# A second order of steps for a gated linear attention followed by a rational feed-forward layer

## The chip, the cores and the metric

One core of one Trainium2 chip. The metric is the device time of one execution in microseconds, lower is better. The profile is of one execution; the other runs are timed without it.

## The reference

The kernel computes an attention with a decaying state, and a two-layer feed-forward network on its output with a rational activation between the layers. Cut to what matters:

```python
# 4 batches x 8 heads, 768 positions, head size 48
f = 1.0 / (1.0 + np.exp(-f_logit))
for t in range(S):
    state = f[:, :, t, :, None] * state + np.einsum('bhd,bhe->bhde', k[:, :, t], v[:, :, t])
    y[:, :, t] = np.einsum('bhd,bhde->bhe', q[:, :, t], state)
x = y.transpose(0, 2, 1, 3).reshape(3072, 384)
h = x @ w_in                                   # 384 -> 2048
P = a[0] + a[1] * h + a[2] * h**2 + a[3] * h**3
Q = 1.0 + np.abs(b[0]) * np.abs(h) + np.abs(b[1]) * h**2
out = (P / (Q + 1e-06)) @ w_out                # 2048 -> 384
```

Inputs and output are float32 in HBM.

## The kernel before

**Units.** The work is cut into 12 units of 256 positions of one batch: unit n is batch n mod 4 and third n div 4 of the sequence. A state is carried from the unit of a batch to its next one, four units on. A step is one piece of work of a unit on one engine. Its name stands first, then the unit, then which part: heads by groups of two, or columns of the 2048 by blocks of 128. A last `@i` is the PSUM slot that a step's output takes; there are four slots of two banks each.

**Steps of the attention half.** `ld n f|k|q|v` loads an input of a unit: f, k and q from the queue of SP as float32 (L200, 384 KB each), v from the queue of POOL, cast to bf16. `ef` and `ls` (ACT, L308 and L313) make the exponential and the logarithm of the gate, `cs` (PE, L323) its sum over positions, `A n 1` and `A n 0` (ACT, L332) the exponentials of that sum, `xa n 1` and `xa n 0` (DVE, L337) multiply k and q by them. `T` (PE, L348) transposes both, `Te` (DVE, L356) reads that out of PSUM, `sc` (PE, L369) makes the scores, `mk` (DVE, L377) masks them, `vm` (POOL, L388; for unit 0 ACT) copies a part of v, `sv` and `id` (PE, L413 to L428) make the new state, `ae` (ACT, L461) and `st` (DVE, L465) finish it, `yb` (PE, L394) makes the output of the attention, and `ye` (ACT, L456) reads it out as the input of the second half.

**Steps of the feed-forward half.** `h` (PE, L474) is the first matmul, in four blocks of 512 columns, each in one PSUM slot. `hy` (ACT, L488) reads it out, `sq` (DVE, L492) or `sa` (ACT, L496) squares it, `ab` (DVE, L500) takes the absolute value. The two terms of Q are added either on PE, `u` (L508) with the logarithm `ln` (ACT, L516) behind it, or by an accumulating transfer from POOL's queue, `zd` (L525) with the logarithm `lz` (ACT, L532). `ex` (ACT, L540) makes 1/Q. `p1`, `p2` and `pm` (DVE, L545, L550, L555) make the pieces of P, which are added by an accumulating transfer from POOL's queue, `ta` (L559), or on DVE, `tv` (L563). `gm` (DVE, L568) multiplies by 1/Q. `o` (PE, L581) is the second matmul, `oe` or, for the last unit, `oc` (L596, L604) reads it out, and `so`, `s0`, `s1` (L590) store it. `wi` and `wo` (POOL's queue, L216, L220) load the weights, cast to bf16; `hv` (DVE, L210) is a small write that `wi` has to wait for. `cz`, `cc`, `ca`, `cb`, `fa`, `fb` make constants.

**What sets the order.** One text, ORDER (from L19), lists all 829 steps, and a loop at the end of the kernel issues them in that order. No scheduler moves them: each engine, and each queue of transfers, runs its own steps in the order in which they stand in the text, and a step waits until its inputs are written and its buffer is free. A step that waits holds up all behind it on its engine or queue. Buffers: three of each of f, k, q and v, two or three of the large arrays of the second half, one of most of the attention's arrays.

Of the kernel before, what the change touches and what calls it, by code (L numbers as in the profile page):

```python
# [19 lines left out]
b1_; cz 0; cb; ca; ld 0 f 2 4; ld 0 f 0 2; ld 0 q 2 4; cc; ld 0 k 2 4; cz 1; ld 0 k 0 2; fa 0  # L20
ef 0 2 4; ld 0 q 0 2; ls 0 2 4; ef 0 0 2; cs 0 2 4 @0; ld 0 v; cz 3; ls 0 0 2; A 0 1 2 4; ld 1 f
cs 0 0 2 @1; cz 2; A 0 0 2 4; A 0 1 0 2; xa 0 1 2 4; A 0 0 0 2; ld 1 k; xa 0 0 2 4; rg; hv 0
xa 0 1 0 2; T 0 2 4 @1; wi 0 4; ld 1 q; xa 0 0 0 2; id 0 0 @0; Te 0 2 4; T 0 0 2 @2; vc 0; ab_
wi 4 8; vm 0 0 s; Te 0 0 2; ae 0; sc 0 0 @2; sc 0 1 @1; sv 0; ef 1; ld 2 f; ld 1 v; ls 1; st 0 0
wi 8 16; mk 0 1; id 0 1; vm 0 1 s; cs 1 @3; mk 0 0; A 1 1; yb 0 0 4 @2; A 1 0; xa 1 1; st 0 1
id 1 0 @3; ye 0; fa 1; ld 2 q; h 0 0 4 @2; ld 2 k; xa 1 0; fb; T 1 @0; hy 0 0 4; h 0 4 8 @1; ae 1
Te 1; sc 1 0 @0; hy 0 4 8; sc 1 1 @2; mk 1 0; ld 3 f; ef 2; sv 1; vm 1 0; sq 0 0 8; ls 2; ld 2 v
cs 2 @0; ab 0 0 8; ld 3 v; mk 1 1; u 0 0 4 @1; A 2 1; vm 1 1; A 2 0; st 1 0; u 0 4 8 @2; p1 0 0 8
ln 0 0 4; id 1 1; h 0 8 12 @0; p2 0 0 8; ld 3 q; ln 0 4 8; pm 0 0 8; yb 1 0 4 @2; ex 0 0 8; xa 2 0
h 0 12 16 @1; st 1 1; ld 3 k; ye 1; tv 0 0 8; hy 0 8 12; h 1 4 8 @2; xa 2 1; hy 0 12 16; vm 2 0  # L30
id 2 0 @0; gm 0 0 8; wo 8 12; hy 1 4 8; sv 2; ld 4 f; vm 2 1; h 1 0 4 @1; sq 0 8 16; ae 2; sa 1 4 8
wo 0 4; wo 4 8; ef 3; p1 0 8 16; h 1 12 16 @2; wo 12 16; hy 1 0 4; st 2 0; ab 0 8 16; vm 3 1; id 2 1
ld 4 q; sa 1 0 4; T 2 @3; ab 1 0 8; vm 3 0; ld 4 v; st 2 1; ls 3; u 1 0 4 @1; Te 2; hy 1 12 16
cs 3 @0; pm 0 8 16; ln 1 0 4; u 0 12 16 @3; A 3 1; sc 2 0 @2; p2 0 8 16; h 1 8 12 @1; A 3 0; mk 2 0
ln 0 12 16; sc 2 1 @0; xa 3 1; u 0 8 12 @2; ld 5 f; hy 1 8 12; ld 4 k; mk 2 1; u 1 4 8 @3; ef 4
id 3 0 @1; ln 0 8 12; ab 1 8 16; yb 2 0 4 @0; xa 3 0; ls 4; sv 3; ld 5 v; p1 1 0 16; ye 2; T 3 @2
ln 1 4 8; o 0 0 0 4 @0; Te 3; ex 0 8 16; cs 4 @3; o 0 1 0 4; tv 0 8 16; h 2 0 4 @2; A 4 0; sq 1 8 16
A 4 1; o 0 1 4 8; sa 2 0 4; gm 0 8 16; h 2 4 8 @3; ld 6 f; ae 3; ld 5 q; hy 2 0 4; pm 1 8 16
o 0 1 8 12; hy 2 4 8; h 2 12 16 @2; pm 1 0 8; ex 1 0 8; st 3 0; o 0 0 4 8; p2 1 0 16; id 3 1
o 0 1 12 16; hy 2 12 16; o 0 0 8 12; st 3 1; ta 1 0 8; sa 2 4 8; xa 4 1; sc 3 0 @1; sc 3 1 @2  # L40
vm 4 1; o 0 0 12 16; ef 5; ld 7 f; mk 3 0; ld 5 k; h 2 8 12 @3; ef 6; mk 3 1; ld 6 q; oe 0 0 2 s
u 1 8 12 @1; hy 2 8 12; ab 2 0 8; yb 3 0 4 @2; xa 4 0; ls 5; u 1 12 16 @3; vm 5 1; ab 2 8 16
ln 1 8 12; vm 4 0; sq 2 8 16; T 4 @0; zd 2 0 8; ln 1 12 16; so 0 0 2; cs 5 @1; ta 1 8 16; ye 3; Te 4
u 2 12 16 @3; A 5 0; p1 2 0 16; sv 4 @0; A 5 1; sc 4 1 @2; ex 1 8 16; h 3 0 4 @1; mk 4 1; ld 6 k
p2 2 0 16; h 3 4 8 @2; hy 3 0 4; gm 1 0 8; ln 2 12 16; id 4 0; u 2 8 12 @1; ae 4; hy 3 4 8; xa 5 0
h 3 12 16 @3; ls 6; st 4 0; xa 5 1; ef 7; id 4 1; ld 8 f; h 3 8 12 @2; st 4 1; hy 3 12 16; pm 2 0 8
sv 5 @0; ln 2 8 12; sc 4 0 @3; id 5 0; ta 2 0 8; hy 3 8 12; mk 4 0; o 1 0 0 4 @1; ae 5; o 1 0 4 8
lz 2 0 8; st 5 0; cs 6 @3; ab 3 0 8; pm 2 8 16; o 1 1 0 4; A 6 0; yb 4 0 4 @2; gm 1 8 16; ta 2 8 16
A 6 1; id 5 1; o 1 1 4 8; ex 2 0 8; sq 3 0 8; o 1 0 8 12; o 1 1 8 12; p1 3 0 16; zd 3 0 8; ye 4
T 5 @3; ld 6 v; ex 2 8 16; st 5 1; h 4 0 4 @2; Te 5; ld 7 v; ld 9 f; ld 7 k; o 1 0 12 16; vm 5 0  # L50
pm 3 0 8; ld 7 q; hy 4 0 4; h 4 4 8 @3; sa 4 0 4; xa 6 0; o 1 1 12 16; ab 3 8 16; sa 4 4 8
h 4 8 12 @2; gm 2 0 8; hy 4 4 8; sq 3 8 16; h 4 12 16 @0; oe 1 0 2 s; hy 4 8 12; gm 2 8 16
o 2 0 0 4 @1; hy 4 12 16; sc 5 0 @2; xa 6 1; sc 5 1 @3; o 2 0 4 8; ls 7; mk 5 0; o 2 1 0 4; lz 3 0 8
cs 7 @0; ab 4 0 8; ld 10 f; u 3 8 12 @2; so 1 0 2; mk 5 1; A 7 1; o 2 1 4 8; ln 3 8 12; p2 3 0 16
yb 5 0 4 @3; A 7 0; sv 6 @2; ab 4 8 16; ld 8 k; ta 3 0 8; ye 5; o 2 0 8 12; pm 3 8 16; ex 3 0 8
# [12 lines left out]
sc 7 0 @2; hy 6 0 4; o 4 0 0 4 @1; mk 7 0; sa 6 0 4; o 4 1 0 4; o 4 0 4 8; mk 7 1; ex 5 8 16; T 8 @3
sq 6 8 16; yb 7 0 4 @0; ls 9; p1 6 0 16; u 6 12 16 @2; ld 10 v; ye 7; lz 5 0 8; o 4 1 4 8; ab 6 0 8
Te 8; o 4 1 8 12; h 7 4 8 @0; ln 6 12 16; pm 6 8 16; ex 5 0 8; h 7 0 4 @3; gm 5 8 16; vm 9 0  # L70
ld 10 q; zd 6 0 8; ld 10 k; o 4 0 8 12; p2 6 0 16; so 3 0 2; hy 7 4 8; o 4 0 12 16; vm 9 1; cs 9 @2
hy 7 0 4; gm 5 0 8; ta 6 8 16; sc 8 1 @0; A 9 0; o 4 1 12 16; sq 7 0 8; A 9 1; h 7 12 16 @3; mk 8 1
oe 4 0 2 s; ef 10; sc 8 0 @2; ld 11 q; sv 8 @1; pm 6 0 8; id 8 0; hy 7 12 16; u 6 8 12 @0; mk 8 0
ls 10; ta 6 0 8; h 7 8 12 @3; ae 8; ln 6 8 12; xa 9 1; cs 10 @2; hy 7 8 12; st 8 0; o 5 0 0 4 @0
ab 7 0 8; ex 6 8 16; yb 8 0 4 @3; xa 9 0; zd 7 0 8; sv 9 @1; sq 7 8 16; id 9 0; ye 8; o 5 1 0 4
p1 7 0 16; ae 9; A 10 0; o 5 1 4 8; ef 11; T 9 @3; st 9 0; ld 11 k; ab 7 8 16; A 10 1; h 8 12 16 @1
Te 9; zd 7 8 16; lz 6 0 8; h 8 8 12 @2; pm 7 8 16; hy 8 12 16; xa 10 1; o 5 0 4 8; hy 8 8 12
sc 9 1 @3; p2 7 0 16; sc 9 0 @1; o 5 1 8 12; so 4 0 2; ls 11; h 8 4 8 @2; mk 9 0; ex 6 0 8
ta 7 8 16; ld 11 v; mk 9 1; o 5 0 8 12; o 5 1 12 16; hy 8 4 8; ab 8 8 16; o 5 0 12 16; sa 8 4 8
# [565 lines left out]
```

## Time and profile before

| what | value |
|---|---|
| median of 3 runs (lowest, highest) | 220.58 us (219.79, 221.02) |
| the profiled execution, its own time | 221.11 us |
| its span in the profile | 219.4 us |
| busy: PE, DVE, ACT, POOL | 201.3, 203.7, 200.7, 76.3 us |
| weight loads of PE | 142.9 us |
| moved by DMA | 42.86 MB, 195 GB/s on average |
| HBM read, written | 25.17 MB, 4.72 MB |

Three engines are busy for 91 to 93% of the span, so a share over the whole span tells little: what matters is where the rest lies, and which wait stands on the way of which engine. The granted TensorE clock is full nearly throughout. Busy PE time counts each matmul from its issue to the end of its pipeline, and is not the same as a full PE. An engine "waits" in this profile when it is idle before an instruction; the name behind the arrow is what ended the wait.

### The profile page before, as it was taken

The page shows a single profiled execution, that of the slowest core. Times are in us where ns is not written, and L with a number is a line of the kernel's source. Part 1 is how long each engine was busy: PE and PEld are TensorE (multiplying, and loading weights), DVE is VectorE, ACT ScalarE, POOL GpSimd, SP SyncE. Part 2 cuts the span into 40 slices and gives each one's busy share as a digit, 9 for nine tenths or more (in the row PEclk, how much of TensorE's full clock was granted, in tenths as well). Part 3 has the DMA queues.
Part 4 walks back from the last instruction along what each step waited for, and adds up shares of the span by engine and source line. Part 5 has one row for each costly group of instructions (what it writes and reads, how often), then busy time and mean ns, then how long its engine had stood idle before and what let it go on. Part 6 is the DMA issues. An engine that isn't in the chain of part 4 may idle for free.

```text
span 219.4 us, 7100 instructions
## 1 busy us (share of the span) xinstructions
PE 201.3 (92%) x3106; PEld 142.9 (65%) x3120; DVE 203.7 (93%) x249; ACT 200.7 (91%) x215; POOL 76.3 (35%) x95
## 2 busy tenths in 40 slices
PE   1569599999999999999999999999999999999991
PEld 1447377567757778577668676786867776865450
DVE  4768999999999999999999999999999999999951
ACT  5554799999999999999999999999999999999980
POOL 4472419020261149362906533123423303231000
PEclk9999999999999999999999999999999999999999
DMA  5999999999999899699999999976978998999515
GB/s 141 266 200 214 225 224 189 207 198 244 268 218 239 226 207 155 129 264 191 214 246 253 215 269 200 214 135 127 193 150 157 193 203 160 187 200 188 112 45 143
DMA packets 62128, 42.86 MB, mean 195 GB/s; under 512 B 51474, under 2 KB 57362, under 8 KB 62098
## 3 DMA queue, kind: packets, MB, share of 16 engines
q0 software_dynamic: 19792, 23.14, 64.3%
q1 hardware_dynamic: 42144, 19.08, 34.8%
q8 instruction: 24, 0.39, 0.7%
q10 hardware_dynamic: 162, 0.20, 0.3%
q14 instruction: 6, 0.05, 0.1%
HBM read 25.17 MB, written 4.72 MB: 136 GB/s over the span
## 4 chain that ended last, share of the span: by engine, by line
PE 40%; ACT 28%; DVE 18%; issue 6%; DMA 2%; SPq 2%; ACTq 0%; DVEq 0%
PE hp L474 15%; PE op L581 13%; ACT hy L488 6%; ACT qi L540 6%; PE y L394 3%; DVE h L492 3%; ACT A L332 3%; ACT h L496 3%; ACT lq L516 3%; DVE gall L568 3%; DVE z L500 2%; PE u L508 2%; DMA fn<-in_f_logit_dram 2%; SPq L200 2%; PE tp L348 2%
## 5 line engine op out<-in xcount | busy, mean ns | idle before, releaser
L581 PE MATMUL op<-w_out_sb,gall 128*128 128x384 bf16 x384 | 69.8, 326 | 0.1
L474 PE MATMUL hp<-xT,w_in_sb 128*128 128x256 bf16 x576 | 68.8, 273 | 0.8 <-ACT xT L456 0.4
L474 PEld LDWEIGHTS <-w_in_sb 128*128 128x128 bf16 x576 | 55.6, 98 | 11.1 <-issue 1.7
L488 ACT CAST hy<-hp 128x1024 bf16<-128x1024 f32 x48 | 49.2, 1063 | 3.3 <-PE hp L474 3.2
L581 PEld LDWEIGHTS <-gall 128*128 128x128 bf16 x384 | 36.2, 98 | 23.4 <-DVE gall L568 1.1
L540 ACT ACTIVATE qi<-lq 128x2048 bf16<-128x2048 f32 (+1 forms) x25 | 46.6, 1888 | 0.1
L559 POOL DMA_DIRECT2D gall<-hy x21 | 20.1, 959 | 66.7 <-DVE gall L555 18.7
L388 POOL COPY vmp<-vn 128x128 bf16<-128x128 bf16 x22 | 26.1, 1198 | 14.3 <-DMA vn<-in_v_dram 10.9
L568 DVE TENSOR_TENSOR gall<-gall,qi 128x2048 bf16<-128x2048 bf16 (+1 forms) x25 | 29.6, 1184 | 1.5 <-ACT qi L540 1.3
L377 DVE TENSOR_TENSOR scm<-sc,mask 128x1024 bf16<-128x1024 f32 x24 | 28.8, 1216 | 0.7 <-PE sc L369 0.5
L555 DVE TENSOR_TENSOR gall<-gall,h 128x2048 bf16<-128x2048 bf16 (+1 forms) x25 | 29.2, 1172 | 0.0
L532 ACT ACTIVATE lq<-z 128x2048 f32<-128x2048 bf16 x13 | 25.5, 1974 | 0.0
L516 ACT ACTIVATE lq<-u 128x1024 f32<-128x1024 f32 x22 | 23.3, 1067 | 0.2 <-PE u L508 0.2
L332 ACT ACTIVATE A<-cs 128x768 f32<-128x768 f32 (+1 forms) x26 | 19.2, 791 | 3.4 <-PE cs L323 3.3
L492 DVE TENSOR_TENSOR h<-hy 128x2048 bf16<-128x2048 bf16 (+1 forms) x18 | 20.9, 1158 | 0.0
L525 POOL DMA_DIRECT2D z<-h x13 | 13.1, 1014 | 21.1 <-ACT osb L596 4.7
L500 DVE TENSOR_SCALAR z<-hy 128x2048 uint16<-128x2048 uint16 (+1 forms) x25 | 17.4, 700 | 0.0
L200 POOL DMA_DIRECT2D vn<-in_v_dram x11 | 12.0, 1095 | 14.5 <-issue 13.9
L545 DVE TENSOR_SCALAR gall<-hy,a_sb 128x4096 bf16<-128x4096 bf16 (+2 forms) x15 | 16.9, 1129 | 0.0
L550 DVE TENSOR_SCALAR hy<-hy,a_sb 128x4096 bf16<-128x4096 bf16 (+2 forms) x15 | 16.8, 1127 | 0.1
L323 PE MATMUL cs<-lsp,Ui 128*128 128x384 bf16 (+1 forms) x39 | 11.1, 345 | 5.7 <-ACT lsp L313 5.7
L356 DVE COPY qkT<-tp 128x2048 bf16<-128x2048 bf16 (+1 forms) x13 | 14.8, 1136 | 1.6 <-PE tp L348 1.6
(70 smaller groups left out, 265.6 us busy)
## 6 DMA issues: line engine op xcount, KB each, us to landing
gall<-hy POOLq DMA_DIRECT2D x21, 512.0 KB, 6.3
z<-h POOLq DMA_DIRECT2D x13, 512.0 KB, 6.4
fn<-in_f_logit_dram SPq DMA_DIRECT2D x11, 384.0 KB, 8.4
kn<-in_k_dram SPq DMA_DIRECT2D x11, 384.0 KB, 6.1
qn<-in_q_dram SPq DMA_DIRECT2D x11, 384.0 KB, 10.7
out_dram<-osb SPq DMA_DIRECT2D x22, 192.0 KB, 3.8
vn<-in_v_dram POOLq DMA_DIRECT2D x11, 192.0 KB, 8.8
w_out_sb<-in_moe_w_out_dram POOLq DMA_DIRECT2D x4, 384.0 KB, 9.5
```

The costliest lines, as they stand in the source:

```text
L332: nc.scalar.activation(t, src, AF.Exp, scale=1.0 if x else -1.0)
L377: nc.vector.tensor_mul(t, s["sc", g].rearrange("s r a i t -> s (r a) (i t)"), mb)
L388: nc.gpsimd.tensor_copy(dst, src)
L474: nc.tensor.matmul(t[:, m - m0, :].rearrange("f (j t) -> f j t", j=UB), w_in_sb[:, kk, m * P:(m + 1) * P], s["x"][:, :, kk, :], start=(kk ...
L488: nc.scalar.copy(fl(big(s, "hy", "hy", 3), m0, m1), fl(s["hp", m0], 0, m1 - m0))
L492: nc.vector.tensor_mul(fl(big(s, "h2", "h2", 2), m0, m1), fl(s["hy"], m0, m1), fl(s["hy"], m0, m1))
L516: nc.scalar.activation(fl(s["lq", g], m0 - 8 * g, m1 - 8 * g), fl(s["u", m0], 0, m1 - m0), AF.Ln, scale=rsig2, bias=1.0 + 1e-6)
L532: nc.scalar.activation(fl(s["lq", g], m0 - 8 * g, m1 - 8 * g), fl(s["z"], m0, m1), AF.Ln, scale=rsig2, bias=1.0 + 1e-6)
L540: nc.scalar.activation(fl(s["qi", g], m0 - 8 * g, m1 - 8 * g), fl(s["lq", g], m0 - 8 * g, m1 - 8 * g), AF.Exp, scale=-1.0)
L555: nc.vector.tensor_mul(fl(s["g"], m0, m1), fl(s["g"], m0, m1), fl(s["h2"], m0, m1))
L568: nc.vector.tensor_mul(fl(s["g"], m0, m1), fl(s["g"], m0, m1), fl(s["qi", g], m0 - 8 * g, m1 - 8 * g))
L581: nc.tensor.matmul(s["op", j][:, 0:DM], s["g"][:, m, C * j:C * j + C], w_out_sb[:, m, :], start=(m == 0), stop=(m == KF - 1))
```

## The change

Only the text ORDER differs. It has the same 829 steps, with the same arguments apart from PSUM slots: 115 of the 157 steps that name a slot have another mark now. Of the steps on an engine's own list, 36 of 221 on DVE, 51 of 215 on ACT and 53 of 260 on PE keep their place. The largest move within a list is 14 places on PE, 13 on ACT, 11 on DVE, 8 on POOL and 6 on SP. The loop, the steps' code, the engines, the buffers and the arithmetic are as they were.

The diff replaces all 87 lines of the text. Its core, by place in the kernel: the start, the loads of units 2 to 7 with their readers, and the steps around the accumulating transfers of units 2 and 3.

```diff
-b1_; cz 0; cb; ca; ld 0 f 2 4; ld 0 f 0 2; ld 0 q 2 4; cc; ld 0 k 2 4; cz 1; ld 0 k 0 2; fa 0
-xa 0 1 0 2; T 0 2 4 @1; wi 0 4; ld 1 q; xa 0 0 0 2; id 0 0 @0; Te 0 2 4; T 0 0 2 @2; vc 0; ab_
-wi 4 8; vm 0 0 s; Te 0 0 2; ae 0; sc 0 0 @2; sc 0 1 @1; sv 0; ef 1; ld 2 f; ld 1 v; ls 1; st 0 0
-wi 8 16; mk 0 1; id 0 1; vm 0 1 s; cs 1 @3; mk 0 0; A 1 1; yb 0 0 4 @2; A 1 0; xa 1 1; st 0 1
...
-Te 1; sc 1 0 @0; hy 0 4 8; sc 1 1 @2; mk 1 0; ld 3 f; ef 2; sv 1; vm 1 0; sq 0 0 8; ls 2; ld 2 v
-cs 2 @0; ab 0 0 8; ld 3 v; mk 1 1; u 0 0 4 @1; A 2 1; vm 1 1; A 2 0; st 1 0; u 0 4 8 @2; p1 0 0 8
...
-ln 0 12 16; sc 2 1 @0; xa 3 1; u 0 8 12 @2; ld 5 f; hy 1 8 12; ld 4 k; mk 2 1; u 1 4 8 @3; ef 4
-id 3 0 @1; ln 0 8 12; ab 1 8 16; yb 2 0 4 @0; xa 3 0; ls 4; sv 3; ld 5 v; p1 1 0 16; ye 2; T 3 @2
-ln 1 4 8; o 0 0 0 4 @0; Te 3; ex 0 8 16; cs 4 @3; o 0 1 0 4; tv 0 8 16; h 2 0 4 @2; A 4 0; sq 1 8 16
-A 4 1; o 0 1 4 8; sa 2 0 4; gm 0 8 16; h 2 4 8 @3; ld 6 f; ae 3; ld 5 q; hy 2 0 4; pm 1 8 16
...
-vm 4 1; o 0 0 12 16; ef 5; ld 7 f; mk 3 0; ld 5 k; h 2 8 12 @3; ef 6; mk 3 1; ld 6 q; oe 0 0 2 s
...
-A 6 1; id 5 1; o 1 1 4 8; ex 2 0 8; sq 3 0 8; o 1 0 8 12; o 1 1 8 12; p1 3 0 16; zd 3 0 8; ye 4
-T 5 @3; ld 6 v; ex 2 8 16; st 5 1; h 4 0 4 @2; Te 5; ld 7 v; ld 9 f; ld 7 k; o 1 0 12 16; vm 5 0
...
+b1_; ca; ld 0 f 2 4; ld 0 f 0 2; ld 0 q 2 4; cb; ld 0 k 2 4; fa 0; ld 0 k 0 2; ef 0 2 4; cz 0
+ld 0 q 0 2; cz 3; ls 0 2 4; ld 0 v; ef 0 0 2; cs 0 2 4 @0; cz 1; rg; ld 1 f; cz 2; ls 0 0 2; ld 1 k
+A 0 1 2 4; cs 0 0 2 @1; A 0 0 2 4; xa 0 1 2 4; id 0 0 @2; A 0 0 0 2; hv 0; xa 0 0 2 4; wi 0 4
+A 0 1 0 2; ld 1 q; ae 0; T 0 2 4 @0; xa 0 1 0 2; xa 0 0 0 2; Te 0 2 4; vc 0; ab_; T 0 0 2 @1; wi 4 8
+vm 0 0 s; sv 0; Te 0 0 2; ld 2 f; cc; st 0 0; ef 1; id 0 1; ld 1 v; sc 0 0 @1; ls 1; sc 0 1 @0
+mk 0 0; wi 8 16; vm 0 1 s; id 1 0 @3; ld 2 q; ld 2 k; mk 0 1; cs 1 @1; yb 0 0 4 @0; A 1 1; xa 1 1
+ye 0; fa 1; A 1 0; h 0 0 4 @0; xa 1 0; ld 3 k; st 0 1; fb; T 1 @1; hy 0 0 4; h 0 4 8 @2; Te 1
+sc 1 1 @1; hy 0 4 8; sc 1 0 @0; mk 1 1; ef 2; sv 1; vm 1 1; sq 0 0 8; ls 2; ld 3 f; vm 1 0; ld 2 v
+ae 1; cs 2 @1; ab 0 0 8; mk 1 0; u 0 0 4 @2; A 2 1; A 2 0; st 1 0; ld 4 f; u 0 4 8 @0; p1 0 0 8
+ln 0 0 4; id 1 1; id 2 0 @1; st 1 1; ln 0 4 8; h 0 8 12 @2; pm 0 0 8; ae 2; ex 0 0 8; ld 3 q
+yb 1 0 4 @0; p2 0 0 8; h 0 12 16 @3; tv 0 0 8; ye 1; xa 2 1; hy 0 8 12; h 1 4 8 @0; gm 0 0 8
+hy 0 12 16; ld 5 k; ld 4 k; h 1 0 4 @2; vm 2 0; hy 1 4 8; p1 0 8 16; ld 3 v; sa 1 4 8; xa 2 0
+h 1 12 16 @3; ld 5 f; wo 0 4; sq 0 8 16; hy 1 0 4; wo 4 8; T 2 @0; ld 4 q; wo 8 12; sa 1 0 4
...
+u 1 4 8 @1; ef 4; xa 3 0; hy 1 8 12; yb 2 0 4 @3; xa 3 1; id 3 0 @2; ls 4; ld 5 v; p1 1 0 16; sv 3
+ae 3; ye 2; ld 7 f; vm 3 1; T 3 @0; ln 1 4 8; st 3 0; cs 4 @3; ab 1 8 16; ef 5; Te 3; id 3 1
+h 2 0 4 @1; A 4 0; sq 1 8 16; A 4 1; o 0 0 0 4 @0; sa 2 0 4; h 2 4 8 @3; st 3 1; xa 4 1; hy 2 0 4
+o 0 1 0 4; pm 1 8 16; ls 5; ld 7 k; sc 3 1 @1; ld 6 k; sc 3 0 @2; hy 2 4 8; o 0 0 4 8; mk 3 1
...
+oe 0 0 2 s; ab 2 0 8; sc 4 1 @1; ex 1 8 16; sv 4 @0; mk 4 1; zd 2 0 8; u 2 12 16 @2; vm 4 1
+pm 2 0 8; h 3 12 16 @1; hy 3 0 4; vm 4 0; vm 5 1; p2 2 0 16; ln 2 12 16; ld 6 v; id 4 0; h 3 4 8 @3
+ae 4; hy 3 12 16; vm 5 0; pm 2 8 16; ta 2 0 8; ls 6; u 2 8 12 @2; xa 5 1; hy 3 4 8; h 3 8 12 @1
...
+ex 2 8 16; p1 3 0 16; yb 4 0 4 @3; o 1 1 8 12; ab 3 8 16; vm 6 0; ex 2 0 8; ta 2 8 16; xa 5 0
+id 5 1; o 1 1 12 16; cs 6 @0; sq 3 8 16; ld 8 q; ld 9 f; o 1 0 8 12; ls 7; ld 7 q; st 5 1
+o 1 0 12 16; ye 4; sq 3 0 8; u 3 8 12 @2; A 6 0; ab 3 0 8; h 4 0 4 @3; oe 1 0 2 s; gm 2 0 8
+zd 3 0 8; A 6 1; T 5 @1; ln 3 8 12; ld 7 v; pm 3 0 8; h 4 4 8 @0; sa 4 0 4; ld 8 f; Te 5; hy 4 0 4
```

On SP's queue the loads from unit 2 on stood as f2 q2 k2 f3 q3 k3 f4 q4 f5 k4 f6 q5 f7 k5 q6. They now stand as f2 q2 k2 k3 f3 f4 q3 k5 k4 f5 q4 f6 f7 k7 k6. On ACT's list ef 5 stood behind sa 2 4 8 and now stands behind ln 1 4 8.

## The prediction

> **What bounds the kernel now.** I first read the page's busy times, then the busy time of each engine by stage, because an average over the span hides where an engine still has air. Each row below is a stretch in us, its length, then busy time and count of PE, PEld, DVE, ACT and POOL, the TensorE clock, the DMA share and GB/s.
>
> ```profile
> 20.00:30.00 10.00, 7.52 (x120) 5.08 (x123) 8.90 (x11) 7.53 (x10) 2.69 (x4) 1.00 1.31 216
> 30.00:40.00 10.00, 9.49 (x188) 7.57 (x189) 10.00 (x13) 10.00 (x13) 6.08 (x9) 1.00 1.14 207
> 40.00:50.00 10.00, 9.64 (x203) 6.28 (x203) 10.00 (x11) 9.52 (x12) 1.33 (x1) 1.00 1.31 200
> 50.00:55.00 5.00, 5.00 (x43) 4.00 (x42) 5.00 (x5) 5.00 (x8) 0.00 (x0) 1.00 1.39 256
> ```
>
> From 30 us on ACT and DVE have no air at all, and the waits of ACT between 30 and 206 us add up to one line:
>
> ```profile
> ACT hy L488 <- PE hp L474: 0.4, 1, 0.4
> ```
>
> DVE has one wait of 0.2 us in the same stretch. So in the middle any order can at best do as well as this one. A gain can come only from the first 30 us (ACT is busy 17.9 of them, DVE 22.2) or from the tail. A loss comes wherever ACT or DVE is made to wait, microsecond for microsecond, since the work behind the wait is as long as before. The end is set by ACT: its last exponentials (ex 11 8 12, ex 11 12 16) end at 212.09, DVE's last two products each wait for them, and from there 7.3 us of the last output sums, copies and stores remain.
>
> The second thing to see in the stage rows is the last two columns: from 5 to 60 us the DMA engines are full (share 1.0 to 1.4, about 200 to 260 GB/s), while q, k, f, v and both weights come in. The queue of SP in that stage, start and length of each issue:
>
> ```profile
> 31.33 2.95 SPq L200 DMA_DIRECT2D fn<-in_f_logit_dram  x1
> 34.37 1.52 SPq L200 DMA_DIRECT2D qn<-in_q_dram  x1
> 35.98 3.95 SPq L200 DMA_DIRECT2D fn<-in_f_logit_dram  x1
> 39.98 5.00 SPq L200 DMA_DIRECT2D kn<-in_k_dram  x1
> 45.08 3.99 SPq L200 DMA_DIRECT2D fn<-in_f_logit_dram  x1
> ```
>
> An issue takes 1.5 to 5 us here, and 0.51 us at the start of the kernel, when nothing is in flight. The landing of the one at 39.98 (k of unit 4), from the view of its tile:
>
> ```profile
> DMA to landing us min/median/max: 13.0/13.0/13.0
> ```
>
> So it lands at 52.98. The same view gives f3 33.96, q3 35.91, f4 43.87, q4 48.92, f5 51.63, k4 52.98, f6 55.76: in the order of issue, each load 384 KB. In this stage a load's landing is set by its place in SP's queue.
>
> **What the Trainium skill says.** "DMA: Bandwidth & Descriptors", section Queues, rings and completion order: each DMA engine takes turns between queue rows packet by packet, and within a ring consumes descriptors in order, though completion is not guaranteed to be in order. The trace agrees with the first part and shows no overtaking on SP's queue. "Perfetto Trace Analysis", section DMA Instruction — HWDGE (DVE, Sync): the profiler starts such an instruction when its semaphores are satisfied. So the 5.00 us above are not a wait for a buffer, but time to place descriptors. "SBUF — State Buffer", section Who interferes with whom: GpSimd shares a port pair with VectorE and is fully blocked while VectorE holds it. The trace agrees: the POOL copies vmp<-vn take 285 ns at the least and 6713 ns at the most.
>
> **The change, part by part.** Steps and instructions are the same; nothing is added or removed, so all is in the waits.
>
> *Head.* On DVE the mask (cc) goes behind Te 0 0 2 into a hole of 1.7 us; fa 0 and the memsets still end before k lands at 7.12, which starts the first xa. On PE, id 0 0 moves ahead of T 0 2 4 (0.5 us out of the way of T 0 0 2, which can start when xa ends at 9.20 instead of 9.71), and sv 0 ahead of sc. The state st 0 0, now at 13.12, can then start near 11.7, but id 0 1 now stands before sc and waits for it; the first mk comes at about 12.8 instead of 13.59: 0.8 us gained. Behind it, ef 2 is at 23.19 and its f2 lands at 22.79, and sv 1 at 23.68 waits for v1, landed at 23.64, issued perhaps 0.4 us earlier because hv moves one step up. So about 0.4 us of it survives: −0.4.
>
> *The load of f5 and its reader, the part that decides.* SP's queue was f3 q3 k3 f4 q4 f5 k4 f6; it becomes k3 f3 f4 q3 k5 k4 f5 q4. All are 384 KB, so the n-th load in the new queue lands when the n-th landed before. Counted from k3 at f3's old place: k3 33.96, f3 35.91, f4 about 40 (k3's landing isn't given), q3 43.87, k5 48.92, k4 51.63, f5 52.98, q4 55.76. The load f5 takes the old place of k4, 1.35 us later than before, since k5, which nobody reads before about 73 us, now stands ahead of it. At the same time its reader ef 5 (ACT, L308) moves from 58.37 us to right behind ln 1 4 8:
>
> ```profile
> 47.91 1.02 ACT L516 ACTIVATE lq<-u 128x1024 f32<-128x1024 f32 x1
> 48.81 1.91 ACT L540 ACTIVATE qi<-lq 128x2048 bf16<-128x2048 f32 x1
> ```
>
> The steps ahead of ef 5 on ACT are exactly those that stood ahead of the second line, and ae 3 besides (0.1 us on the queue). On the old clock ACT reaches ef 5 at 48.81 + 0.1 = 48.9, with the head's gain at 48.5. The data is there at 53.0. ACT stands still for about 4.5 us, and everything behind it is 53.0 − 48.9 = 4.1 us later than in the old order; the head's gain is swallowed by the wait. Queued behind ef 5 on ACT are A 4 0 and A 4 1, sa 2 0 4, hy 2 0 4 and ls 5. DVE waits for A 4 1 in xa 4 1: on the old clock it gets there at 49.69 (place of tv 0 8 16) + st, sq, st (0.47 + 1.13 + 0.47) = 51.8; A 4 1 ends near 53.0 + 0.73 + 0.69 + 0.8 = 55.2. DVE loses 3.4 us, so it doesn't shield the loss, and PE waits for the PSUM slots that ACT and DVE have not read. Nothing later gives it back: ACT's air behind this place is the 0.4 us above, of which none lies behind 49 us.
>
> Bounds of this term: if f5 behaved like the median load of its kind (8.4 us after an issue at 39.98: 48.4), there is no wait. If v3, which POOL now issues only after vm 2 0 (about 33 us instead of 24.84), shifts the sharing between the two queues by its own 1.4 us either way, f5 lands at 51.6 to 54.4, and the term is +2.7 to +5.5. I take +4.1, since total bytes ahead of f5 are those ahead of k4 before: v1 to v4 and both weights in any case.
>
> *Other loads.* f3 (35.91) is read by ef 3, which moves behind sa 1 0 4, at about 37.5: margin 1.2 to 1.6. q3 (43.87) is read by xa 3 0 at about 44.5. k4 (51.63) and q4 (55.76) come before their readers, once A 4 1 is late. No cost.
>
> *Accumulating transfers.* zd 3 0 8 was issued at 80.39 and is read by lz 3 0 8 at 89.69. Seven DVE steps (6.9 us) now stand ahead of its input ab 3 0 8, at 75.78 before: it is issued near 83.4, lands after the same 6.36 us at 89.8, and is wanted at 90.6 (ln 3 8 12 is now ahead). A margin of 2.9 us becomes 0.8; z<-h lands after 5.5 to 11.1 us, median 6.4. zd 2 0 8 and ta 4 8 16 have 1 to 1.5 us. I take +0.2, bounds 0 and +2.
>
> *Tail.* The last four ACT steps, the last DVE steps and the last PE sums keep their order: 0.
>
> Sum on the profiled execution: 221.11 (its span 219.4, and 1.7 around it) + 4.1 + 0.2 = 225.4. The median of the runs is 0.53 below the profiled one: 220.58 + 4.3 = **224.9 us**.
>
> **Rivals.** (a) *f5 is in time* — not slower. If SP's loads land by their lag from issue rather than by place, or HBM loads speed up enough, f5 is there by 48.5; it has to come 4.5 us earlier than k4 did. Then the head's 0.4 is left, less 0.2: 220.4. For it: issues at 51 us and later land within 8 us. Against it: every load issued between 19 and 45 us took 10.7 us or more. Faster by over 0.5% would need 1.1 us, more than the head gives. (b) *POOL's queue on top*: vm 6 0 now stands between ta 2 0 8 and ta 2 8 16, waits for v6 (issued near 69.5, landing after 6.7 to 9 us) and can be held by DVE for up to 6.7 us. With both at their worst ta 2 8 16 is issued near 85 instead of 79, lands 6.3 us later, gm 2 8 16 (about 87) waits 4 us, and zd 3 0 8 is held up behind it: 224.9 + 4 = 229. Against it: the median such copy takes 0.64 us. (c) *Order drifts little*: both gates ease (f5 lands near 51, a margin holds), 222.
>
> **How the numbers follow.** My forecast 0.72, with its own range 223.2 to 226.8; (a) 0.12; (b) 0.10; (c) 0.06. The range leaves out (a) and the far half of (b): 221.8 to 228.0. About 0.5% (1.1 us) is what a measurement of this kernel tells from no change: faster (below 219.5) 0.04, from (a) with a larger head gain; same (to 221.7) 0.10; slower 0.86.
>
> **What would show it.** Right: a wait of ACT of 3.5 to 5.5 us at L308 for the DMA of fn, near 49 us; DVE waiting about 3.5 us at L337 for A; PE air beside it; from 55 us on ACT without gaps; the f5 load landing at 51.5 to 54.5; the last ex ending near 216. Wrong: no wait at L308 beyond 1 us, which makes (a); or waits of ACT at L532 or of DVE at L568 for z<-h or gall<-hy of several us, with a long POOL copy ahead of them, which makes (b).

## The result and the profile after

The changed kernel takes 223.0 us (median of five runs), the kernel before 220.81 us in the same comparison: a ratio of 1.0104, 95% interval 1.0069 to 1.0139. Executions more than 1.5% above the fastest of their kernel, such as one of these five (228.84 us) and the profiled one of experiment e2 (225.26 us), are left out of all ratios. The forecast was 224.9, with 221.8 to 228.0 as its range and 0.86 on slower. The time is inside the range, 1.9 us below the forecast and 0.2 us below the likeliest case's own range. The profiled execution took 224.19 us with a span of 222.5, against 219.4 before.

The same four stretches as in the prediction, of the kernel after (stretch, length, then busy time and count of PE, PEld, DVE, ACT, POOL, the clock, the DMA share, GB/s):

```profile
20.00:30.00 10.00, 7.94 (x121) 5.86 (x121) 8.43 (x14) 6.72 (x9) 1.39 (x3) 1.00 1.19 226
30.00:40.00 10.00, 9.81 (x186) 7.84 (x184) 9.97 (x12) 10.00 (x13) 6.31 (x9) 1.00 1.12 195
40.00:50.00 10.00, 9.88 (x203) 6.43 (x203) 10.00 (x12) 9.13 (x13) 2.17 (x2) 1.00 1.32 200
50.00:55.00 5.00, 2.93 (x26) 2.28 (x24) 3.42 (x5) 3.64 (x5) 0.00 (x0) 1.00 1.35 232
```

From 50 to 55 us there is air on all of PE, DVE and ACT, where before there was none: DVE fell from 5.00 to 3.42 us, ACT from 5.00 to 3.64. From 20 to 30 us ACT does 0.8 us less than before. The clock's column shows 1.00 also where its record says nothing. The record begins at 17.54 us in the kernel before and at 22.05 us after, and the work ahead of that ran at half speed: in the kernel before, the matmuls of `cs` start 0.32 us apart at 14 us and 0.16 us apart at 25 us. So the granted clock was not full in the head of either kernel.

The places where ACT stood, from its timeline (start, length, engine, line, operation, and in brackets the idle time ahead of it and what ended it), and DVE at xa 4 1:

```profile
51.36 0.84 ACT L308 ACTIVATE fn<-fn 128x768 f32<-128x768 f32 x1 [1.95 <-DMA fn<-in_f_logit_dram]
94.07 1.91 ACT L532 ACTIVATE lq<-z 128x2048 f32<-128x2048 bf16 x1 [1.05 <-DMA z<-h]
```

```profile
53.64 0.96 DVE L337 TENSOR_TENSOR qkp<-kn,A 128x768 bf16<-128x768 f32 x1 [1.58 <-ACT A L332]
```

The first is ef 5 waiting for f5, the third DVE waiting for A 4 1 behind it: the mechanism of the forecast, at the place named, but 1.95 us long and not 4.5. The second is lz 3 0 8 waiting for the accumulating transfer zd 3 0 8, which the forecast had with a margin of 0.8 us. The queue of SP in the stage before, as it now ran:

```profile
31.61 3.14 SPq L200 DMA_DIRECT2D kn<-in_k_dram  x2
34.83 3.63 SPq L200 DMA_DIRECT2D fn<-in_f_logit_dram  x1
38.52 5.23 SPq L200 DMA_DIRECT2D qn<-in_q_dram  x1
```

The load at 34.83 is f5. It landed 16.5 us later, at 51.34.

The head went the other way than forecast. The start of ex 0 0 8 on ACT, before and then after:

```profile
29.54 1.91 ACT L540 ACTIVATE qi<-lq 128x2048 bf16<-128x2048 f32 x1
```

```profile
30.34 1.91 ACT L540 ACTIVATE qi<-lq 128x2048 bf16<-128x2048 f32 x1
```

It is 0.8 us later, though the first mask product had started at 12.33 us instead of 13.59. The groups of the first matmul (count: shortest, median, longest duration in ns; first and last start), from 15 to 25 us, before and after:

```profile
L474 PE MATMUL hp<-xT,w_in_sb x24: 269/272/273, 18.4 to 22.0; 128*128 128x256 bf16 x24
```

```profile
L474 PE MATMUL hp<-xT,w_in_sb x24: 272/392/421, 17.4 to 23.1; 128*128 128x256 bf16 x24
```

So h 0 0 4 began 1.0 us earlier and then ran at half speed: 2.72 us instead of 1.47, since full speed came at 22.05 us and not at 17.54. Beside it fa 1 waited 1.04 us on DVE for b, and xa 1 0 behind it started at 19.09 us instead of 18.86.

### The profile page after: what moved, and what is told of

Its sections match the earlier page's. It is cut to its first block, busy times and chain, and to the rows that moved or that the text cites. A ratio compares the mean times of both kernels' runs of the same rounds, so it can differ in the third digit from the quotient of the medians.

```text
span 222.5 us, 7112 instructions
## 1 busy us (share of the span) xinstructions
PE 204.8 (92%) x3120; PEld 144.9 (65%) x3120; DVE 203.9 (92%) x249; ACT 200.2 (90%) x215; POOL 72.4 (33%) x95
## 4 chain that ended last, share of the span: by engine, by line
PE 51%; DVE 25%; ACT 11%; DMA 5%; issue 5%; SPq 1%; ACTq 0%; DVEq 0%
PE op L581 19%; PE hp L474 16%; PE tp L348 4%; DVE scm L377 4%; PE y L394 4%; PE u L508 4%; DMA z<-h 3%; DVE h L492 3%; DVE qkp L337 3%; DVE gall L555 3%; DVE z L500 2%; DVE gall L545 2%; DVE state L465 2%; ACT qi L540 2%; ACT hy L488 2%
## 5 line engine op out<-in xcount | busy, mean ns | idle before, releaser
L474 PE MATMUL hp<-xT,w_in_sb 128*128 128x256 bf16 x576 | 69.7, 276 | 3.8 <-ACT A L332 2.1
L474 PEld LDWEIGHTS <-w_in_sb 128*128 128x128 bf16 x576 | 56.5, 99 | 14.8 <-issue 4.9
L559 POOL DMA_DIRECT2D gall<-hy x21 | 26.0, 1322 | 70.2 <-ACT hy L488 38.6
L388 POOL COPY vmp<-vn 128x128 bf16<-128x128 bf16 x22 | 16.9, 936 | 18.9 <-DMA vn<-in_v_dram 13.8
L525 POOL DMA_DIRECT2D z<-h x13 | 15.6, 1200 | 20.6 <-DVE h L492 9.4
L200 POOL DMA_DIRECT2D vn<-in_v_dram x11 | 14.7, 1338 | 17.1 <-issue 14.3
L500 DVE TENSOR_SCALAR z<-hy 128x2048 uint16<-128x2048 uint16 (+1 forms) x25 | 16.7, 672 | 0.0
```

The source lines that it names most:

```text
L474: nc.tensor.matmul(t[:, m - m0, :].rearrange("f (j t) -> f j t", j=UB), w_in_sb[:, kk, m * P:(m + 1) * P], s["x"][:, :, kk, :], start=(kk ...
L559: nc.gpsimd.dma_start(out=fl(s["g"], m0, m1), in_=fl(s["hy"], m0, m1), accum_op=ALU.add)
```

## The experiments

All ratios are to the kernel before on the same chip, with their 95% interval. The diffs show the pieces of the text ORDER around each moved step. A gate is a place in an engine's list where it waits for one transfer. The theory after the result was: the early reader ef 5 costs (gate 1), and the rest comes from zd 3 0 8 (gate 2) and from the head.

**e1: the reader put back.**

```diff
-ln 1 4 8; st 3 0; cs 4 @3; ab 1 8 16; ef 5; Te 3; id 3 1
+ln 1 4 8; st 3 0; cs 4 @3; ab 1 8 16; Te 3; id 3 1
-o 0 1 0 4; pm 1 8 16; ls 5
+o 0 1 0 4; pm 1 8 16; ef 5; ls 5
```

> The changed order with one step put back: ef 5 stands directly ahead of ls 5 on ACT (behind hy 2 0 4) instead of ahead of A 4 0; every other step of the change stays. Theory (the early reader costs): in the changed kernel ACT stood 1.95 us at ef 5 from 49.41 us and DVE 1.58 us at xa 4 1 for A 4 1. With the step back ACT reaches it about 3 us later, behind the landing of f5 at 51.3; both waits go, and the time falls by 1.6 to 2.0 us, to about 221.2, ratio to the kernel before near 1.002. Rival (the wait is only where a loss shows that something earlier makes; the air moves on to the next waits): the wait at ef 5 goes, but ACT or DVE wait about as long further on, and the time falls by less than 0.5 us.

Measured: 223.45 us, ratio 1.0116 (1.0078 to 1.0155). Nothing was gained. The wait at ef 5 is gone, and ACT stands longer at gate 2:

```profile
93.54 1.91 ACT L532 ACTIVATE lq<-z 128x2048 f32<-128x2048 bf16 x1 [2.55 <-DMA z<-h]
```

The rival was right here: zd 3 0 8 is issued 2.1 us earlier than in the first profile of after (84.10 instead of 86.21), but lands 0.5 us earlier only. Its way from issue to landing in this kernel and in the kernel before:

```profile
L525 POOL DMA_DIRECT2D z<-h x1: 849/849/849, 84.1 to 84.1; - x1
DMA to landing us min/median/max: 9.3/9.3/9.3
```

```profile
L525 POOL DMA_DIRECT2D z<-h x1: 853/853/853, 80.4 to 80.4; - x1
DMA to landing us min/median/max: 6.4/6.4/6.4
```

**e2: the reader's move alone, on the kernel before.**

```diff
-ln 1 4 8; o 0 0 0 4 @0; Te 3
+ln 1 4 8; ef 5; o 0 0 0 4 @0; Te 3
-o 0 0 12 16; ef 5; ld 7 f; mk 3 0
+o 0 0 12 16; ld 7 f; mk 3 0
```

> The kernel before with one step of the change alone: ef 5 directly behind ln 1 4 8 on ACT, ahead of ex 0 8 16, A 4 0 and A 4 1. SP's queue stays f3 q3 k3 f4 q4 f5 k4 f6. Theory: ACT arrives at 48.8, f5 lands at 51.63, so ACT waits 2.8 us and the time rises by 2.3 to 2.8 us, to about 223.3, ratio 1.010 to 1.013: this one step is enough for the whole loss. Rival (the order of the loads is what costs, not the reader): no wait over 1 us, ratio 0.998 to 1.004.

Measured: 222.9 us, ratio 1.0096 (1.0073 to 1.0119), 2.1 us. The waits of ACT have one new line of weight:

```profile
ACT fn L308 <- DMA fn<-in_f_logit_dram: 2.9, 1, 2.9
```

Forecast 2.8 us of wait, measured 2.9: f5 landed at 51.20 us. The profile is of an execution of 225.26 us, 2.4 above the median, and a stretch of TensorE at half speed behind this wait adds to it (last section); the wait itself lies ahead of that. With SP's queue as it was, the reader's move by itself costs about what the whole change costs. The expected 2.3 to 2.8 us reach into the upper end of the interval (1.6 to 2.6 us); the rival, that the order of the loads costs, is out, since the loads did not move.

**e3: f5 ahead of k5 in SP's queue.**

```diff
-hy 0 12 16; ld 5 k; ld 4 k
+hy 0 12 16; ld 5 f; ld 5 k; ld 4 k
-h 1 12 16 @3; ld 5 f; wo 0 4
+h 1 12 16 @3; wo 0 4
```

> The changed order with one load moved: f5 ahead of k5 on SP's queue, so k3 f3 f4 q3 f5 k5 k4 q4. The reader ef 5 stays where the change has it. Theory (a load lands by its place in the queue): f5 takes the place that k5 had, whose load landed at 42.5 us, ACT finds it there at 49.4, the wait at ef 5 goes and the time falls by 1.6 to 2.0 us, to about 221.2. k4 keeps its place. Rival (landing goes by the lag from the time of issue and by what shares the DMA engines): f5 moves forward by less than 4 us, a wait of ACT of over 0.5 us at L308 is left or another load (k4, read by xa 4 1 near 52 us) is late in its stead, and the time falls by less than 1 us.

Measured: 223.5 us, ratio 1.0146 (1.0115 to 1.0177). The load did what the place in the queue says: issued at 33.19, landed at 43.33, where k5 had landed at 42.51. ACT no longer waits at ef 5. The time did not fall: ACT waits 2.45 us at lz 3 0 8, as in e1. In this execution the head was another 1.3 us later as well (see the last section), so its profile can't be compared further.

**e4: the changed kernel once more.**

> The changed kernel as it is, to see what of its head repeats. In its first profile the first matmuls of h 0 0 4 came every 214 ns from 17.4 to 19.7 us, against 109 ns in the kernel before, and ACT waited 4.4 us for two hp tiles against 2.8 us. Theory (the longer idle stretch of TensorE ahead of h 0 0 4, 0.94 us against 0.45 us, belongs to the order): the slow matmuls are there again, within about 1 us of the same place, and ACT waits 4 us or more at L488. Rival (where TensorE turns fast is chance from execution to execution): the place moves by 2 us or more, and the wait at L488 may be 3 us or less. The wait at ef 5 is 1.5 to 2.5 us in both.

Measured: ratio 1.0110 (1.0069 to 1.0151). Its waits of ACT:

```profile
ACT hy L488 <- PE hp L474: 3.4, 3, 2.4
ACT lq L532 <- DMA z<-h: 2.5, 1, 2.5
ACT osb L604 <- PE op L581: 2.0, 2, 1.0
ACT fn L308 <- DMA fn<-in_f_logit_dram: 1.7, 1, 1.7
```

Gate 1 repeats (1.95, 1.72 us). Gate 2 is 2.5 us here against 1.05 in the first profile, with a lag of 9.3 against 7.8 us. The rival was right on the head: full speed came at 16.46 us, all 24 matmuls of the head took 269 to 273 ns, and ex 0 0 8 started at 29.51, no later than in the kernel before. Where TensorE turns fast is not fixed by the order.

**e5, e7: the loads f8 and f10 out of the way of zd 3 0 8,** with ef 5 back (e5) and alone (e7). In the changed order f8 and f10 are issued at 83 to 86 us, around zd 3 0 8; in the kernel before SP issues no load from 74 to 89 us.

```diff
-sa 4 0 4; ld 8 f; Te 5
+sa 4 0 4; Te 5
-hy 4 8 12; ld 10 f; sc 5 0 @0
+hy 4 8 12; sc 5 0 @0
-ld 9 k; A 7 1
+ld 9 k; ld 8 f; ld 10 f; A 7 1
```

> As e1 (the changed order with ef 5 put back ahead of ls 5), and besides the loads f8 and f10 moved on SP's queue to behind k9, which waits for a buffer until about 94 us; nothing else. In e1 ACT waited 2.55 us at lz 3 0 8 for the accumulating transfer zd 3 0 8 (issued 84.10, landed 93.45) while f8, f10 and v7 were in flight. Theory (two gates in a row: the first wait only hid part of the second, and the lag of zd 3 0 8 comes from the loads that the change moved into its time): zd 3 0 8 lands within 7.2 us of its issue as in the kernel before (6.4), the wait at lz 3 0 8 falls under 0.6 us, and the time is 1.8 to 2.6 us below e1, about 220.6, ratio 0.999 to 1.003. Rival (the lag comes from POOL's own queue, with ta 2 8 16 ahead and v7 behind, and not from SP's loads): the lag stays above 8.5 us, the wait above 1.5 us, the time within 0.6 us of e1.

> The changed order with the two loads f8 and f10 moved behind k9 alone; ef 5 stays early. Theory (two gates in a row): the wait at ef 5 stays at 1.7 to 2.0 us and the one at lz 3 0 8 falls under 0.3 us; the end moves by 0.8 to 1.6 us against the changed kernel, to about 221.7, between e5 and the changed kernel. Rival (one of the two gates alone sets the time): as fast as e5 within 0.4 us, or as slow as the changed kernel within 0.4 us.

Measured: e5 222.39 us, ratio 1.0088 (1.0063 to 1.0113); e7 223.28 us, ratio 1.0126 (1.0097 to 1.0155). The transfer in e5:

```profile
L525 POOL DMA_DIRECT2D z<-h x1: 849/849/849, 85.0 to 85.0; - x1
DMA to landing us min/median/max: 7.1/7.1/7.1
```

7.1 us in e5 and 7.4 in e7, against 9.3 in e1 and e4. So the two loads in its time lengthen the lag, and not POOL's own queue, whose order is the same. They are not all of it: with them away the lag was 7.9 us in e9 (below), as long as the 7.8 with them in the first profile of after. The waits of ACT behind 20 us in e5:

```profile
ACT hy L488 <- PE hp L474: 4.6, 2, 2.5
ACT osb L604 <- PE op L581: 2.0, 2, 1.0
ACT A L332 <- PE cs L323: 0.8, 1, 0.8
ACT lq L532 <- DMA z<-h: 0.3, 1, 0.3
```

The first and the third lie ahead of 28 us, the second behind the last exponential. Between them ACT has 0.3 us at gate 2 and two waits as small. But the time is not that of the kernel before, which the expectation had: the last exponentials are still 1.45 us later in the profile, and 1.32 of that was already there at ex 0 0 8. In e7 the profile has 0.49 us at ef 5 and 0.58 us at gate 2, and its execution took 222.36 us; the four other runs behind the ratio, at 222.77 to 223.69 us, do not show the gain. By its time e7 is as slow as the changed kernel, which is what its rival said.

**e6: the input of zd 3 0 8 earlier,** on the order of e1.

```diff
-ex 2 8 16; p1 3 0 16
+ex 2 8 16; sq 3 0 8; ab 3 0 8; p1 3 0 16
-ye 4; sq 3 0 8; u 3 8 12 @2; A 6 0; ab 3 0 8; h 4 0 4 @3
+ye 4; u 3 8 12 @2; A 6 0; h 4 0 4 @3
```

> As e1, and besides sq 3 0 8 and ab 3 0 8 put ahead of p1 3 0 16 on DVE, so that the input of zd 3 0 8 is ready about 4 us earlier; POOL's queue keeps its order (vm 6 0, ta 2 8 16, zd 3 0 8), so zd 3 0 8 can be issued at about 82.3 instead of 84.10. Theory (the landing of zd 3 0 8 is the gate that sets the end): the wait at lz 3 0 8 falls from 2.55 to 0.6 to 1.2 us and the time by 1.3 to 1.9 us against e1, to about 221.2. Rival (the wait there is air that comes back elsewhere, as the one at ef 5 did in e1): time within 0.6 us of e1. Cost to look for: ab 3 8 16 and sq 3 8 16 come 1.9 us later, and u 3 8 12 and ln 3 8 12 with them.

Measured: 223.54 us, ratio 1.0157 (1.0117 to 1.0196): the expected gain did not come. In the profile zd 3 0 8 is issued at 81.32 and lands at 90.83, and no wait at gate 2 is left; but ACT waits 0.42 us for u 3 8 12 and 0.78 us for three blocks of h behind it, and DVE 1.05 us for T 5. In this profile the last exponentials are 0.97 us earlier than in e1, so the cost named in the expectation took a part of the gain; the timed runs (223.54 us, against 223.45 in e1) show none of it, as the rival said.

**e9, e10: the wait for b in the head,** on e5 and alone. In six of the seven profiles of the changed head so far fa 1 waited 0.7 to 2.0 us on DVE for b (the coefficients of Q in the reference), with xa 1 0 and T 1 behind it.

```diff
-ye 0; fa 1; A 1 0; h 0 0 4 @0; xa 1 0; ld 3 k; st 0 1; fb; T 1 @1; hy 0 0 4; h 0 4 8 @2; Te 1
+ye 0; A 1 0; h 0 0 4 @0; xa 1 0; ld 3 k; st 0 1; fa 1; T 1 @1; hy 0 0 4; h 0 4 8 @2; Te 1; fb
```

> As e5 (ef 5 put back, f8 and f10 behind k9), and besides in the head on DVE fa 1 moved from ahead of xa 1 0 to behind st 0 1, and fb to behind Te 1. In e5 ACT had almost no wait left behind 30 us (0.28 us at lz 3 0 8, 0.25 us at A 7 0) and its profile still ended 1.4 us later than that of before; ex 0 0 8 already started 1.31 us later. In e5 fa 1 waited 1.66 us for b (landed 18.8), with xa 1 0, T 1 and h 0 4 8 behind it. Theory (the rest of the loss is the head, and of it most is the wait for b): xa 1 0 starts 1.2 us earlier, hy 0 4 8 and ex 0 0 8 0.7 to 1.2 us earlier, and the time falls by as much against e5, to about 221.4, ratio 1.002 to 1.006. Rival (the head's loss is TensorE at half speed, wherever fa 1 stands): under 0.3 us against e5, ratio 1.007 to 1.010.

> The changed order with fa 1 behind st 0 1 and fb behind Te 1 alone; both gates stay. Theory: the head's gain of 0.7 to 1.2 us is swallowed where the landing of f5 sets ACT's time, unless SP's queue moves forward with the head; half of it or more is gone by the end: 222.3 to 223.1, ratio 1.008 to 1.012. Rival (DVE and ACT move up as a whole, loads too): 221.6 to 222.1, ratio 1.005 to 1.007.

Measured: e9 221.91 us, ratio 1.0072 (1.0044 to 1.0101); e10 223.43 us, ratio 1.0135 (1.0096 to 1.0175). The wait for b is gone and the head gained nothing: ex 0 0 8 starts at 30.87 and 30.40. In both executions TensorE turned fast only at 22.5 and 21.95 us. The matmuls of the head in e9:

```profile
L474 PE MATMUL hp<-xT,w_in_sb x24: 273/346/417, 18.2 to 23.7; 128*128 128x256 bf16 x24
```

By the profile the rival of e9 was right; the interval of its ratio takes in both expectations. The ratio of e10 is above both of its expectations, which took a gain of the head for granted. In e10 f5 landed at 48.84, before ACT came to ef 5 at 49.4, so gate 1 was open without being touched, and gate 2 kept ACT for 2.27 us: gate 1 is 0 to 2 us wide from execution to execution, and gate 2 was wider here than in the first profile of after (1.05), though not than in e4 (2.52).

**e8, e11, e12: TensorE kept busy in the head.** `wm k` issues k matmuls of 512 columns on a zeroed tile (L304), `zw` zeroes it (L271); both stand unused in the kernel.

```diff
 # e8, on before
+zw; cz 0 ... wm 7 @3; cs 0 2 4 @0 ... wm 4 @3; T 0 2 4 @1
+wm 1 @3; sc 0 0 @2 ... wm 1 @3; id 0 1
 # e11, on before
+zw; cz 0 ... wm 4 @3; cs 0 2 4 @0 ... wm 2 @3; T 0 2 4 @1
 # e12, on e9
+zw; fa 0 ... wm 4 @3; cs 0 2 4 @0 ... sv 0; wm 1 @3
-id 1 0 @3; ld 2 q
+ld 2 q
+wm 1 @3; cs 1 @1; yb 0 0 4 @0; id 1 0 @3
```

> The kernel before with 13 matmuls on a zeroed tile added in holes of TensorE of the head (7 ahead of the first cs, 4 ahead of T 0 2 4, one ahead of sc 0 0, one ahead of id 0 1), and one memset for them on DVE; the results of these matmuls are read by nobody. In the profile of before TensorE ran at half speed until 17.54 us. Theory (half speed in the head costs, and it ends once TensorE has been busy): full speed from 7 to 11 us on, h 0 0 4 starts 0.6 to 1.2 us earlier; of it 0.3 to 0.5 us reach ef 2 and the end, since f2 and v1 land at 22.8 and 23.6: ratio 0.996 to 1.000. Rival (full speed comes when it comes, and the added matmuls hold up the real ones): ratio 1.000 to 1.004.

> The kernel before with 6 matmuls on a zeroed tile in the head (4 ahead of the first cs, 2 ahead of T 0 2 4) instead of the 13 of e8, and the memset for them; nobody reads their results. In e8 the head gained 1.08 us at ex 0 0 8, and three stretches of 0.85, 1.16 and 0.89 us in which TensorE stood for nothing that the profile shows (ahead of 34.9, 51.5 and 114.1 us) took it away. Theory (these stretches depend on where the instructions come to lie, not on the work): with 6 they are gone or others, and the head gains 0.5 to 1.0 us; ratio 0.995 to 0.999. Rival (any added instruction of TensorE ahead brings them): ratio 1.008 or more, with stretches of about 1 us again.

> As e9, and besides 6 matmuls on a zeroed tile (4 ahead of the first cs, one behind sv 0, one in the place of id 1 0 ahead of cs 1), with id 1 0 moved behind yb 0 0 4, and a memset for them; nobody reads their results. In the changed kernel TensorE ran at half speed until 22.05 us in the first profile and until 16.5 us in the second. Theory (with TensorE busy early it runs at full speed from 11 us on in every execution): h 0 0 4 takes 1.5 us instead of up to 2.7, and the time is 0.5 to 1.2 us below e9, about 220.5, ratio 0.997 to 1.002. Rival (stretches without cause as in e8): ratio 1.006 or more.

Measured: e8 ratio 1.0135 (1.0082 to 1.0188), e11 1.0040 (1.0012 to 1.0068), e12 222.23 us, ratio 1.0055 (1.0026 to 1.0084). With 13 matmuls full speed came at 9.43 us, and ex 0 0 8 came 1.08 us earlier than in the profile of before, 0.56 us earlier than in that of e2, whose head is the same; so half speed in the head costs about half a microsecond to one. The ratio is above what either expectation of e8 had: the gain was lost again on PE, which stood three times for nothing that the profile shows; one of them:

```profile
51.51 0.82 PE L581 MATMUL op<-w_out_sb,gall 128*128 128x384 bf16 x4 [1.16 <-issue]
```

The profiles of kernels without added matmuls have no such wait of PE; those with six have two each, smaller ones (0.36 and 0.76 us in e11, 0.52 and 0.20 in e12). So the rival of e11 was right that added instructions bring them, though not that they come to as much again: e11 with 1.12 us of them costs 0.4%, and its six matmuls bought no gain, since full speed came only at 21.15 us. In e12 it came at 17.62 us, and ex 0 0 8 at 29.75, 1.1 us earlier than in e9. At the last exponentials 0.8 us of that is left, though the wait at gate 2 of e9 is gone too, and the ratio misses its forecast and overlaps that of e9. No version beat the kernel before.

## Why the prediction was right, and what in it was wrong

From the profiles, ACT's clock at two places: ex 0 0 8 near 30 us, and the first of the last two exponentials (210.09 before, whose own waits between are 0.4 us). All in us:

| profile | ex 0 0 8, against before | wait at ef 5 | wait at lz 3 0 8 | last exponentials, against before |
|---|---|---|---|---|
| after, first | +0.80 | 1.95 | 1.05 | +2.97 |
| after, again (e4) | −0.03 | 1.72 | 2.52 | +4.15 |
| e1 (ef 5 back) | +0.46 | 0 | 2.55 | +2.97 |
| e3 (f5 first) | +2.09 | 0 | 2.45 | +4.50 |
| e7 (f8, f10 late) | +0.78 | 0.49 | 0.58 | +1.14 |
| e5 (both) | +1.32 | 0 | 0.28 | +1.45 |
| e9 (both, fa 1 late) | +1.33 | 0 | 1.15 | +1.93 |
| e10 (fa 1 late) | +0.86 | 0 | 2.27 | +2.23 |

The three columns add up to 0.0 to 0.9 us more than the last one; 0.4 of that is the wait that the kernel before had itself. In e6 and e12 both gates are open, and the waits of ACT lie elsewhere (the last exponentials are +2.00 and +1.16). The first column has an error of its own: in e2, with the head of the kernel before, ex 0 0 8 came 0.52 us earlier than in the profile of before.

- **What bounds it (right).** That a gain could come only from the head or the tail, and a loss wherever ACT is made to wait, is what every row shows: the end follows the head and the waits. It does so not quite microsecond for microsecond, as the forecast had it, but up to 0.9 us short of it.
- **The load of f5 and its reader (mechanism right, size too large).** Forecast 4.1 us net, measured waits of 1.95 and 1.72, between the sign named for right (3.5 to 5.5 us) and the one for wrong (no more than 1 us). The mis-sized terms are both of the subtraction: f5 landed at 51.34 and 50.52, not 52.98, and ACT came at 49.41 and 48.83, not 48.5. The n-th place was a good rule for order (e3: f5 in k5's place landed 0.8 us from where k5 had) and not exact in time: SP reached f5 at 34.83 us, while k4 in the same place had been issued at 39.98, and POOL's loads came later (the last piece of w_out landed at 53.18 instead of 48.32); that the one made room for the other is not shown. In the same place f5 landed at 48.84 in e10. In the case against this term, the reading that loads issued at 51 us and later land within 8 us holds for this stage only: q9, issued at 105.07 us, took 14.85. My lower bound of +2.7 was itself too high. DVE's loss was forecast at 3.4 and was 1.58.
- **Which part of the change it is (right, with one addition).** e2 shows that the reader's move is enough for a loss of 2.1 us. It is not needed for it: in e1 it is undone and nothing comes back.
- **Accumulating transfers (wrong: +0.2, measured 1.05 and 2.52).** I took the lag of 6.36 us over from the kernel before, where SP issued no load from 74 to 89 us. The step that failed is that I counted the DVE steps in front of zd 3 0 8 and not the loads that SP's new order issues beside it. With f8 and f10 away the lag is 6.9 to 7.9 (e5, e7, e9, e12), with them 7.8 to 9.5.
- **The head (wrong sign: −0.4, measured −0.03 to +2.1).** The chain on DVE and PE did move up as worked out (the first mk 1.26 us earlier). It was then lost on h 0 0 4, which met TensorE at half speed in seven of the nine profiles that have the changed head without added matmuls (full speed from 20.29 us or later), while the two with the old head have full speed from 17.54 and 17.14. In the other two, e4 and e7, it came by 17.0; e7 lost its 0.78 us with 1.40 us of wait for b. Two profiles are too few to say that the old head is safe from half speed: with six matmuls added (e11) it had full speed only from 21.15. I did not price the clock at all.
- **Tail 0 (right),** and the rival of a long POOL copy ahead of ta 2 8 16 did not occur in its size: the copy took up to 2.6 us, and DVE waited at most 0.7 us for that transfer. The rival in which f5 is in time occurred in e10, where only fa 1 and fb stand elsewhere, and did not save the time, because gate 2 stood behind it: I had treated the two as adding, and they partly replace one another in after and e1, while in e4 they did add.
- **The sum.** The forecast adds 4.3 us, nearly twice the 2.3 us of the ratio (3.1 between the two profiled executions). That it came no further off is in part luck: one term was too large and two too small. The forecast of slower was sound, its division was not.

**What stays open.** With gate 1 gone and gate 2 eased (e5, e9, the latter with 1.15 us left there) the ratios are 1.0088 and 1.0072, the changed kernel 1.0104 and 1.0110: the intervals overlap, so the timed runs don't prove the gain that the profiles show, and e7 shows none. The one loss that a moved step alone brings in the timed runs is that of e2; how the loss of the whole change divides between the two gates and the head is read from single profiles. What is left in e5's profile is the head's 1.3 us; that the old head would take it away was not tried, since the two heads take different PSUM slots all through. e12 gained 1.1 us there in its profile and no time beyond the error.

## What to carry to other kernels

Where two engines have no air, look for every wait that a new order can open, and treat waits on one engine as gates in a row: in e1, e3 and e10 the first was open, the wait stood at the second, and no time came back. For a transfer that is waited for, take its lag from a stretch with the same transfers beside it, not from its own row under the old order. A hole in TensorE's work ahead of a matmul can cost more than the hole, when the clock falls.

## What the runs showed of the hardware that I had not expected

TensorE's speed is switched in steps of time. In the record of the clock every stretch at half speed inside a run is 3.41 us long, and every stretch at full speed between the switches on either side of it is a whole multiple of that (75.09 = 22 of them in e1, 81.92 = 24 in e4, 68.27 = 20 in e3). Each of the seven follows a stretch of the same length in which PE was busy for 1.9 us at most. In e1, right behind the wait at gate 2 (busy time of PE first, the clock behind POOL):

```profile
93.00:96.41 3.41, 1.58 (x91) 1.13 (x90) 3.41 (x5) 2.87 (x3) 0.55 (x2) 1.00 1.33 204
96.41:99.83 3.42, 3.42 (x41) 1.86 (x41) 3.38 (x5) 3.42 (x4) 3.42 (x3) 0.50 1.13 280
```

PE was busy 1.58 of 3.41 us, and the next 3.41 us ran at half speed. The same came behind 1.60 us in e4 and 0.52 in e2, and in the head of e3 (behind 1.34 us, from 27.1 to 30.5), where DVE waited for the state of unit 1:

```profile
30.80 0.56 DVE L465 TENSOR_TENSOR state<-sv,alast 128x384 bf16<-128x384 f32 x1 [1.63 <-PE sv L424]
```

Little work alone does not bring it: behind 1.57 us in e4 (from 50.59 us) and 1.51 us in e7 (from 16.97 us) full speed went on. The first profile of after had no such stretch, and e1 with the shorter waits ended no earlier than it. "TensorE: Matmul & The Clock Gate" of the Trainium skill, section Part 1: The HAM clock gate (the "warmup" mystery), says that half clock is the default, that full clock takes about one busy window of 3413 ns, and that the window runs freely and doesn't start with the kernel. The runs agree in the length, and in the last point too: the same order turned fast at 22.05 us in one execution and at 16.46 in another, 5.6 us apart and so more than one such stretch. How much work makes a stretch busy enough they leave open: in the kernel before, PE was busy 2.92 us in the stretch ahead of full speed, and in the kernel after, 3.14 us from 11.81 to 15.23 were followed by more half speed.

The second thing is PE's waits for its own issue in the three kernels with added matmuls: 0.85, 1.16 and 0.89 us in e8 with 13 of them, 1.12 and 0.72 us in all in e11 and e12 with six, none in the nine other profiles of these experiments and the two kernels as they were. Each ends 2.2 to 2.7 us behind the start of a fetch of instructions by the DMA engines; but such fetches are in all profiles, mostly without a wait, so the cause is not shown.
